# Attention pieces regrouped from six to five a batch, SyncE's transfers put in given order, K's transpose ahead of Q's, in a fused Linformer attention and feed-forward kernel

## The chip, the cores and the metric

One core of one Trainium2 chip. The metric is device time in microseconds (us) of one launch. The kernel before takes 488.2 us (median of four runs, 488.0 to 488.4). Two figures for one kernel below, such as 488.2 and 485.8 us, are the device time and the span of the profile, from the first to the last instruction; times inside a profile count from the start of its span. Each experiment was compared with the kernel before on the same chip and in the same rounds, so ratios are safer to compare than times of different experiments.

In the views, PE is TensorE (matrix products) and PEld its weight loads, DVE is VectorE, ACT is ScalarE. POOL (PoolE) and SP (SyncE) here mainly issue transfers, which 16 DMA engines carry out. "Issue" is the time for which the issuing engine is held; a transfer "lands" when its data has arrived.

## The reference

```python
# q, k, v: (8 batches, 8 heads, 1024, 64); E, F: (64, 1024); w_in: (512, 2048); w_out: (2048, 512)
k_proj = einsum('ks,bhsd->bhkd', E, k)          # 1024 positions -> 64
v_proj = einsum('ks,bhsd->bhkd', F, v)
attn   = softmax(q @ k_proj.T / sqrt(64))       # per head
x      = (attn @ v_proj), heads joined          # (8192, 512)
out    = relu(x @ w_in)**2 @ w_out              # (8192, 512)
```

## The kernel before

Each batch goes through two chunks of the feed-forward network: `f0` (16 steps of the first layer), `s0` (15 steps of the second), `f1`, `s1`, so 62 steps numbered n = 0 to 61. Batch 0 runs `f0 f1 s0 s1`. The second layer's matrix product uses 7 products with sums and differences (`s0` to `s3`, `T1` to `T4`) in place of 8. Attention of the next batch (`nxt`) is cut into pieces, and tables say before which step each piece is put:

```python
ORDERED = {mybir.EngineType.PE, mybir.EngineType.DVE, mybir.EngineType.Activation}
...
qkv_pool = ctx.enter_context(tc.tile_pool(name="qkv", bufs=1))     # one Q_sb, one K_sb, one V_sb
qt_pool  = ctx.enter_context(tc.tile_pool(name="qt", bufs=1))      # one qT
aps = ctx.enter_context(tc.tile_pool(name="aps", bufs=2, space=bass.MemoryType.PSUM))
...
def transpose_q(self):      # "Q's crossbar": a DMA transpose of 1 MB, SBUF to SBUF, issued by SyncE
    nc.sync.dma_start_transpose(out=self.qT[:], in_=self.Q[:].rearrange("p h c -> p (h c)"))
def copy_kp(self):          # after project(): two copies on VectorE, then "K's transpose", a small one
    ...
    nc.sync.dma_start_transpose(out=self.kT[:], in_=self.kp[:].rearrange("k h a d -> k (h a d)"))
...
with tc.manual_schedule(engines=ORDERED):
    def load_batch(b):      # three loads of 1 MB each on PoolE's queue
        if b < B:
            tiles = [load(n, src, b) for n, src in (("Q_sb", q), ("K_sb", k), ("V_sb", v))]
            return Attention(b, *tiles)
```

Engines in `ORDERED` get their instructions in the order in which the program names them. The others, here SyncE and PoolE, get the order that the scheduler of the kernel language settles when the kernel is built. Each of Q_sb, K_sb and V_sb has one buffer. So a batch's load of Q waits until the batch before has had its Q read by the crossbar, and its loads of K and V wait until the batch before has been projected on TensorE.

The softmax here doesn't subtract the row's maximum and nothing guards it: scores larger than these inputs give would overflow.

## Time and profile before

| | before |
|---|---|
| device time, median | 488.2 us |
| TensorE busy | 472.6 of 485.8 us |
| a middle batch | 57.60 us, TensorE busy throughout |
| the last batch, without attention | 55.7 us with the tail |

From the page of the kernel before: the span, the busy time of each engine, then TensorE's busy share and granted clock, in tenths, in 40 equal slices.

```profile
span 485.8 us, 8378 instructions
...
PE 472.6 (97%) x3614; PEld 292.3 (60%) x3614; DVE 315.4 (65%) x380; ACT 262.4 (54%) x414; POOL 33.2 (7%) x46
...
PE   4899999999999999999999999999999999999997
...
PEclk9999999999999999999999999999999999999999
```

The next view is the table of stretches: bounds, length, busy us (and instruction count) of the engines, the granted clock, the DMA share and GB/s. The rows are the end of batch 0, batch 1, and one middle batch.

```profile
core 0: us, PE busy (x) PEld busy (x) DVE busy (x) ACT busy (x) POOL busy (x), PEclk, DMA share, GB/s
52.00:83.48 31.48, 30.67 (x305) 23.37 (x305) 19.16 (x29) 13.75 (x20) 2.62 (x3) 1.00 0.99 171
83.48:143.75 60.27, 60.01 (x451) 36.56 (x449) 38.37 (x46) 33.61 (x52) 5.26 (x6) 1.00 0.87 155
201.35:258.95 57.60, 57.60 (x434) 35.56 (x432) 38.80 (x45) 31.94 (x50) 2.63 (x3) 1.00 0.53 106
```

First the timeline of SyncE, start and length of the issue of each transfer:

```profile
57.73 5.02 SPq L167 DMA_TRANSPOSE qT<-Q_sb  x1
62.81 1.25 SPq L185 DMA_TRANSPOSE kT<-kp  x1
...
79.29 12.77 SPq L167 DMA_TRANSPOSE qT<-Q_sb  x1
```

Then PoolE, with the idle time ahead of each issue and what ended it:

```profile
66.84 0.87 POOL L78 DMA_DIRECT2D Q_sb<-in_q_dram  x1 [34.43 <-DMA qT<-Q_sb]
67.70 0.88 POOL L78 DMA_DIRECT2D K_sb<-in_k_dram  x1
68.57 0.89 POOL L78 DMA_DIRECT2D V_sb<-in_v_dram  x1
96.24 0.88 POOL L78 DMA_DIRECT2D Q_sb<-in_q_dram  x1 [26.78 <-DMA qT<-Q_sb]
```

Batch 2's Q stands first in PoolE's queue and waits for batch 1's crossbar, and K and V stand behind it. Whether by intent or not, this keeps all three loads off the DMA engines while batch 1's crossbar runs. The DMA view of 57.7 to 66.4 us, the life of that crossbar, shows this: queue, packets and MB, share of the 16 DMA engines' time; then the crossbar's time from issue to landing.

```profile
q1 hardware_dynamic: 4672, 1.18, 85.9%
...
qT<-Q_sb SPq DMA_TRANSPOSE x1, 8.6
```

SyncE's queue (q1) has the DMA engines to itself, and the crossbar lands in 8.6 us. Last, TensorE at the first scores of batch 1, which need qT and kT:

```profile
65.19 1.03 PE L461 MATMUL ps_y<-T,hsq 128*128 128x256 bf16 x8
66.72 0.63 PE L201 MATMUL ps_att<-qT,kT 64*64 64x512 bf16 x8 [0.51 <-DMA kT<-kp]
```

The wait there is 0.5 us, and it is for kT, which SyncE issues behind Q's crossbar.

### The profile page before, as it was taken

To read this page: it belongs to the slowest core of one execution; us is meant where nothing else is said; L and a number is where in the kernel's file an instruction comes from. 1 tells how busy PE (TensorE), PEld (TensorE's weight loads), DVE (VectorE), ACT (ScalarE), POOL (GpSimd) and SP (SyncE) were. 2 spreads that over 40 slices of the span, in tenths; PEclk is the share of its full clock that TensorE was granted. 3 is DMA by queue.
4 is the path that set the end of the run, shared out by engine and by line. 5 is a ranking of instruction groups with operands and counts; after the bars stand their busy time and mean duration, and the time that the engine had idled before them with its cause. 6 is when DMAs were issued, how large, how long until landed. Compare 5 with 4: busy or idle time off the path is not lost.

```text
span 485.8 us, 8378 instructions
## 1 busy us (share of the span) xinstructions
PE 472.6 (97%) x3614; PEld 292.3 (60%) x3614; DVE 315.4 (65%) x380; ACT 262.4 (54%) x414; POOL 33.2 (7%) x46
## 2 busy tenths in 40 slices
PE   4899999999999999999999999999999999999997
PEld 2444677475574845757475665747557474666656
DVE  2478855566848568495765848566694856848383
ACT  2487445665727556355655467264672746645351
POOL 6330020010020000100010000200000000000000
PEclk9999999999999999999999999999999999999999
DMA  9999999997389124991149921893232102020202
GB/s 162 204 205 206 164 144 219 235 170 178 46 145 226 30 88 86 172 187 44 44 89 194 162 88 20 141 220 66 88 74 68 45 0 88 2 88 0 88 0 88
DMA packets 72501, 55.46 MB, mean 114 GB/s; under 512 B 33936, under 2 KB 64656, under 8 KB 72464
## 3 DMA queue, kind: packets, MB, share of 16 engines
q0 software_dynamic: 30336, 29.36, 38.5%
q1 hardware_dynamic: 42128, 25.56, 20.7%
q8 instruction: 28, 0.46, 0.4%
q14 instruction: 9, 0.07, 0.0%
HBM read 59.24 MB, written 16.78 MB: 156 GB/s over the span
## 4 chain that ended last, share of the span: by engine, by line
PE 85%; DMA 10%; ACT 2%; POOL 1%; issue 1%; DVE 0%; POOLq 0%; DVEq 0%
PE ps_h L441 39%; PE ps_y L461 23%; PE ps_z L461 11%; DMA V_sb<-in_v_dram 7%; PE ps_x L461 5%; DMA w_in<-in_moe_w_in_dram 2%; PE ps_att L216 2%; PE ps_kv L175 2%; PE ps_att L201 2%; DMA kT<-kp 1%; ACT h_relu L492 1%; PE ps_kv L176 0%; POOL K_sb L91 0%; DVE hsq L500 0%; ACT hsq L498 0%
## 5 line engine op out<-in xcount | busy, mean ns | idle before, releaser
L441 PE MATMUL ps_h<-xT,w_in 128*128 128x512 bf16 x1024 | 225.0, 379 | 0.2 <-DMA w_in<-in_moe_w_in_dram 0.2
L500 DVE TENSOR_TENSOR hsq<-h_relu 128x1024 bf16<-128x1024 f32 x123 | 150.2, 1222 | 67.4 <-ACT h_relu L492 66.8
L492 ACT ACTIVATE h_relu<-ps_h 128x512 f32<-128x512 f32 x256 | 150.6, 597 | 66.2 <-PE ps_h L441 65.7
L441 PEld LDWEIGHTS <-w_in 128*128 128x128 bf16 x1024 | 99.5, 98 | 118.2 <-issue 1.8
L461 PEld LDWEIGHTS <-s 128*128 128x128 bf16 x1024 | 98.4, 98 | 19.6 <-issue 8.1
L461 PEld LDWEIGHTS <-hsq 128*128 128x128 bf16 x768 | 73.2, 98 | 19.4 <-issue 3.0
L461 PE MATMUL ps_y<-T,s 128*128 128x256 bf16 x512 | 62.4, 273 | 0.1
L574 DVE TENSOR_TENSOR o_sb<-ps_z,p_b 128x512 f32<-128x512 f32 x16 | 11.1, 692 | 52.9 <-issue 25.7
L455 DVE TENSOR_TENSOR s<-hsq 128x1024 bf16<-128x1024 bf16 x64 | 43.6, 684 | 0.0
L570 ACT COPY o_sb<-ps_y 128x512 f32<-128x512 f32 x15 | 8.8, 585 | 55.4 <-PE ps_y L461 55.4
L235 DVE TENSOR_TENSOR xT<-ps_att,rs 128x1024 bf16<-128x1024 f32 x28 | 33.0, 1217 | 7.3 <-ACT rs L229 7.3
L461 PE MATMUL ps_y<-w_out,hsq 128*128 128x256 bf16 x256 | 34.5, 273 | 0.3 <-DVE hsq L500 0.3
L461 PE MATMUL ps_x<-w_out,hsq 128*128 128x256 bf16 x256 | 33.2, 273 | 0.0
L461 PE MATMUL ps_y<-T,hsq 128*128 128x256 bf16 x256 | 31.7, 272 | 0.0
L208 ACT ACTIVATE expT<-ps_att 128x1024 bf16<-128x1024 f32 x28 | 27.4, 1028 | 6.4 <-PE ps_att L201 6.4
L461 PE MATMUL ps_z<-T,s 128*128 128x256 bf16 x256 | 30.8, 273 | 0.0
L461 PE MATMUL ps_z<-w_out,s 128*128 128x256 bf16 x256 | 30.6, 273 | 0.0
L570 ACT COPY p_b<-ps_y 128x512 f32<-128x512 f32 (+1 forms) x17 | 9.5, 560 | 28.1 <-PE ps_y L461 28.0
L78 POOL DMA_DIRECT2D Q_sb<-in_q_dram x7 | 6.1, 876 | 263.2 <-DMA qT<-Q_sb 262.8
L574 DVE TENSOR_TENSOR o_sb<-ps_y,p_d 128x512 f32<-128x512 f32 (+1 forms) x17 | 11.2, 660 | 19.2 <-PE ps_y L461 19.2
L228 ACT ACTIVATE rs<-ps_att 128x1024 f32<-128x1024 f32 x14 | 14.3, 1023 | 14.6 <-PE ps_att L216 14.6
L455 DVE TENSOR_TENSOR s<-s,hsq 128x1024 bf16<-128x1024 bf16 x32 | 21.9, 687 | 0.5
(74 smaller groups left out, 239.3 us busy)
## 6 DMA issues: line engine op xcount, KB each, us to landing
out_dram<-o_sb SPq DMA_DIRECT2D x30, 512.0 KB, 3.3
K_sb<-in_k_dram POOLq DMA_DIRECT2D x7, 1024.0 KB, 17.3
V_sb<-in_v_dram POOLq DMA_DIRECT2D x7, 1024.0 KB, 22.4
Q_sb<-in_q_dram POOLq DMA_DIRECT2D x7, 1024.0 KB, 9.6
w_in<-in_moe_w_in_dram POOLq DMA_DIRECT2D x8, 256.0 KB, 13.7
w_out<-in_moe_w_out_dram POOLq DMA_DIRECT2D x4, 512.0 KB, 13.2
K_sb<-in_k_dram POOLq DMA_DIRECT2D x2, 512.0 KB, 7.8
V_sb<-in_v_dram POOLq DMA_DIRECT2D x2, 512.0 KB, 12.7
```

The source lines that it names most:

```text
L175: nc.tensor.matmul(ps[0:KP, :], lhsT=ET[:, i, :], rhs=kv[:, :, i, :], start=f, stop=l)
L201: nc.tensor.matmul(ps[o, bank, :], lhsT=self.kT[r, 2 * pr + j, :], start=True, stop=True, rhs=self.qT[r, NT * (2 * pr + j):NT * (2 * pr + ...
L208: nc.scalar.activation(e[:], self.ps["s", pr][:], AF.Exp, scale=SCALE)
L228: nc.scalar.activation(rs[:], self.ps["r", g][:], AF.Ln)
L235: nc.vector.tensor_tensor(out=self.xT[:, 2 * g + e].rearrange("p a n t -> p a (n t)"), in0=self.ps["v", g, e][:], in1=self.rs[g][:], op=AL ...
L441: nc.tensor.matmul(ps[:], lhsT=w_in_blk(cb, fb), rhs=xT[:, cb, :, 2 * ch:2 * ch + 2], start=(cb == 0), stop=(cb == NCB - 1),)
L455: nc.vector.tensor_tensor(out=s[o][:, js], in0=x, in1=y, op=op)
L461: nc.tensor.matmul(ps[tb] if len(ps) == 2 else ps[0][:, tb], lhsT=lhs[:, j, tb * P:(tb + 1) * P], rhs=rhs[:, j], start=first and n == 0 an ...
L492: nc.scalar.activation(r[:, n], ps[:], AF.Relu)
L500: multiply = lambda: nc.vector.tensor_tensor(out=o, in0=r[:], in1=r[:], op=ALU.mult)
L570: nc.scalar.copy(to[:, t], ps)
L574: nc.vector.tensor_tensor(out=to[:, t], in0=ps, in1=more[:, t], op=ALU.add)
```

## The change

Its intent: fewer switches between attention and feed-forward on TensorE; K's small transpose ahead of Q's large one; Q's crossbar after its load, at a place that the program gives. SyncE joins the engines in given order. The core of the diff, with cuts marked:

```diff
-ORDERED = {mybir.EngineType.PE, mybir.EngineType.DVE, mybir.EngineType.Activation}
+ORDERED = {
+    mybir.EngineType.PE, mybir.EngineType.DVE, mybir.EngineType.Activation, mybir.EngineType.SP,
+}
...
     PIECES = {
-        0: "transpose_q", 1: "copy_kp", 2: "copy_vp", 4: "copy_v_down",
-        24: "scores 0, scores 1, exponentials 0", 25: "exponentials 1",
-        27: "sums 0, values 0 0, reciprocals 0", 30: "values 0 1", 31: "normalize 0 0", 32: "normalize 0 1",
-        47: "scores 2, scores 3, exponentials 2", 48: "exponentials 3",
-        50: "sums 1, values 1 0, reciprocals 1", 53: "values 1 1", 54: "normalize 1 0", 55: "normalize 1 1",
+        1: "copy_kp", 2: "copy_vp", 4: "copy_v_down",
+        20: "scores 0, scores 1, exponentials 0", 21: "exponentials 1",
+        23: "sums 0, values 0 0, reciprocals 0", 26: "normalize 0 0",
+        28: "scores 2, scores 3, exponentials 2", 29: "exponentials 3",
+        47: "values 0 1, sums 1, reciprocals 1", 48: "normalize 0 1",
+        53: "values 1 0, values 1 1", 54: "normalize 1 0", 55: "normalize 1 1",
     }
     BATCH_1 = {
-        32: "project", 33: "copy_kp, transpose_q, copy_vp", 36: "copy_v_down",
+        33: "project", 34: "copy_kp, transpose_q, copy_vp", 37: "copy_v_down",
         46: "scores 0, scores 1, exponentials 0", 47: "exponentials 1",
...      # the rest of batch 1's pieces regrouped: seven places become six
-    BATCH_2 = {**PIECES, 1: "", 2: "", 4: "", 9: "project", 10: "copy_kp", 11: "copy_vp", 14: "copy_v_down"}
+    BATCH_2 = {
+        **PIECES, 1: "", 2: "", 4: "", 9: "project", 10: "copy_kp, transpose_q", 11: "copy_vp", 14: "copy_v_down",
+    }
     SECOND_HALF = {
-        1: "last_of_first", 7: "second_half 0 0", 9: "second_half 1 0, second_half 0 1",
+        1: "last_of_first", 7: "second_half 0 0", 9: "second_half 1 0", 10: "second_half 0 1",
...
                     if n == (35, 12, 1)[min(b, 2)]:
                         ahead = load_batch(b + 2)
+                    if b and n == 33 and ahead:
+                        ahead.transpose_q()
...      # also: one more held-back square in batch 0, later operand sums on VectorE
```

## The prediction

> **What bounds the kernel now.** TensorE: 97% of the 485.8 us span by the page, 85% of the chain that ended last, at clock 0.999. In the table of stretches the middle batches take 57.60 us, TensorE busy for all of it; VectorE (38.8) and ScalarE (31.9) have room. The last batch, without attention, takes 2 x 26.1 us, so attention costs 5.4 us a batch. Its matmuls account for 3.9 us (projection 1.73, scores 0.86, sums and values 1.30, start to start in the timeline). The other 1.5 us is changes of tile shape: 8 second-layer matmuls take 0.87 us alone and 0.96-0.98 beside a piece, so about 0.11 us a change, 13 a batch. The Trainium skill ("TensorEngine Tiling (Array Packing)", Key Properties) says that changing the tiling mode drains TensorE; the 0.1 us agrees in kind.
>
> **What the change does.**
> 1. Six attention places a batch become five ("values 0 1" joins "sums 1"; both "values" of group 1 and the next projection stand together): 13 changes of shape become 11, 0.23 us x 6 batches = 1.4 us. Batch 1 goes from seven places to six: 0.2.
> 2. Batch 1's projection comes one step later. Now TensorE stands 0.4 us there, at 52.0-52.7, for V's load (timeline). Gone.
> 3. Batch 1: SyncE now issues Q's crossbar (57.7, 5.0 us of issue) ahead of K's (62.8), and the scores wait for kT until 66.7: 0.5 us. With K first, kT lands near 60 and Q's crossbar, still bound by Q's load, near 65, a microsecond before it is wanted. Gone.
> 4. Opening batch: the second transposes of Q wait 0.4 us for Q's load at 29.8; a step later this goes, for one more change of shape: 0.3 net.
> 5. Costs. (a) Batch 2: Q's crossbar follows K's at about 95.7, takes 7 us to land, and the scores come four steps earlier, at about 102.3: waits 0.4 (0 to 0.8). (b) Scores 3 needs the PSUM buffer that "normalize 0 0" frees, which stands on VectorE behind an addition: free 2.1 us after p3's end, wanted at 2.06: 0.1 x 6. (c) Batch 1: "sums 1" waits for exponentials 3 behind a copy on ScalarE, "values 1 1" for "normalize 0 1": 0.5 together.
> 6. Q is loaded and turned half a batch earlier. PoolE's 263 us of waiting for the crossbar is off the chain; scores have 5 us to spare for kT (median landing 10.5): nothing.
> The reordered operands move VectorE work that has slack: nothing.
>
> Gains 1.4 + 0.2 + 0.4 + 0.5 + 0.3 = 2.8; costs 0.4 + 0.6 + 0.5 = 1.5; net 1.4 with rounding.
>
> **Prediction.** 486.7 us, 8 in 10 between 485.0 and 488.4. Faster by over 2%: 0.01; within 2%: 0.97; slower: 0.02.
>
> **What the profile would show.** Middle batches at 57.4-57.5 us, TensorE still busy throughout; five attention places a batch; in batch 1 no wait of the projection for V nor of the scores for kT, K's transpose issued first; a short wait of scores for qT in batch 2; perhaps a weight load of scores waiting for normalize once a batch. PoolE's wait stays large.
>
> **What would make it wrong.** SyncE in given order: a transpose waiting for a late load blocks the output stores, and through the two output buffers the additions, PSUM and TensorE. A crossbar amid loads, as at 79.3 now (12.8 us of issue), before batch 2's or 3's scores. More PSUM waits than I found: every batch then gives back more than its 0.23 us.

## The result

The changed kernel takes 511.0 us (median of four, 509.8 to 511.5) against 488.2 us: a ratio of 1.0464, 95% interval 1.0444 to 1.0484. A ratio here is the mean time of one kernel's fast runs over that of the other's of the same rounds, so not quite the ratio of the medians quoted. The prediction was 486.7 us, so it was wrong in direction and by far more than its range.

The page of the changed kernel:

```profile
span 509.5 us, 8379 instructions
...
PE 475.6 (93%) x3614; PEld 295.0 (58%) x3614; DVE 313.5 (62%) x380; ACT 263.1 (52%) x414; POOL 33.2 (7%) x46
...
PE   4899919991999999999999999999999999999997
...
PEclk9999967996999999999999999999999999999999
```

The loss is not spread: two slices of TensorE are nearly empty, in batches 0 and 1, and the clock dips beside each. The other slices look as before. The table of stretches, for the same stretches of work (the end of batch 0, batch 1, one middle batch; columns as in the table above):

```profile
52.00:96.00 44.00, 33.53 (x309) 24.54 (x307) 19.95 (x30) 13.91 (x20) 2.63 (x3) 0.84 0.88 146
96.00:168.72 72.72, 61.37 (x451) 37.10 (x449) 38.06 (x46) 33.92 (x52) 5.26 (x6) 0.93 0.73 131
226.10:283.48 57.38, 57.38 (x435) 35.64 (x432) 38.52 (x45) 32.13 (x50) 2.63 (x3) 1.00 0.59 113
```

Batch 0 ends 12.5 us later (96.00 against 83.48), and batch 1 takes 12.5 us longer (72.72 against 60.27). The middle batch takes 57.38 in place of 57.60 us: the regrouping gives what it was meant to give. Four such batches give 0.9 us and batch 6, from start to start in the chain of waits, gives 0.4 (398.41 to 453.94, against 374.33 to 430.22), so 12.5 + 12.5 - 1.3 = 23.7 us, which is the difference of the spans (509.5 - 485.8).

TensorE at the first scores of batch 1:

```profile
65.13 1.03 PE L467 MATMUL ps_y<-T,hsq 128*128 128x256 bf16 x8
76.43 1.07 PE L203 MATMUL ps_att<-qT,kT 64*64 64x512 bf16 x8 [10.26 <-DMA qT<-Q_sb]
77.43 1.89 PE L467 MATMUL ps_y<-T,hsq 128*128 128x256 bf16 x8
79.11 1.91 PE L467 MATMUL ps_y<-w_out,hsq 128*128 128x256 bf16 x8
...
126.08 1.07 PE L203 MATMUL ps_att<-qT,kT 64*64 64x512 bf16 x8 [11.09 <-DMA qT<-Q_sb]
```

TensorE reaches the same place at the same time as before (65.13 and 65.19 us) and then stands 10.3 us for qT; at batch 2's first scores it stands 11.1 us. Behind each wait the matmuls are slow: 8 of the second layer take 1.7 us from start to start, where they took 0.9. SyncE and PoolE, in that order:

```profile
57.64 1.74 SPq L187 DMA_TRANSPOSE kT<-kp  x1
59.51 14.74 SPq L169 DMA_TRANSPOSE qT<-Q_sb  x1
...
107.06 1.26 SPq L187 DMA_TRANSPOSE kT<-kp  x1
108.50 15.52 SPq L169 DMA_TRANSPOSE qT<-Q_sb  x1
```

```profile
55.68 0.88 POOL L80 DMA_DIRECT2D K_sb<-in_k_dram  x1 [22.68 <-PE ps_kv L178]
56.55 0.88 POOL L80 DMA_DIRECT2D V_sb<-in_v_dram  x1
76.85 0.88 POOL L80 DMA_DIRECT2D Q_sb<-in_q_dram  x1 [19.42 <-DMA qT<-Q_sb]
106.07 0.88 POOL L80 DMA_DIRECT2D K_sb<-in_k_dram  x1 [28.35 <-PE ps_kv L178]
107.14 0.89 POOL L80 DMA_DIRECT2D V_sb<-in_v_dram  x1 [0.20 <-issue]
```

SyncE issues Q's crossbar only 1.8 us later than before (59.51 against 57.73), but the issue lasts 14.7 us in place of 5.0. What is new is on PoolE, which the diff does not name: K and V of batch 2 go off at 55.7 and 56.6 us, as soon as the projection of batch 1 has read their buffers, where they used to go at 67.7 and 68.6 us, behind Q. The same happens for batch 3 at 106 us. The DMA view of 59.5 to 76.4 us, the life of this crossbar:

```profile
q0 software_dynamic: 1876, 1.89, 73.8%
q1 hardware_dynamic: 4829, 1.50, 49.8%
...
qT<-Q_sb SPq DMA_TRANSPOSE x1, 16.8
```

PoolE's loads (q0) and SyncE's transfers (q1) are now on the DMA engines together, and the crossbar lands in 16.8 us in place of 8.6. The Trainium skill ("DMA: Bandwidth & Descriptors", Issuing engines are not separate DMA queues) says that transfers started by different engines run on the same 16 DMA engines and interleave; these two views agree.

The built queues show the order of the loads on PoolE for batches 1 to 4:

```
before:   K V Q | Q K V | Q K V | Q K V
changed:  K V Q | K V Q | K V Q | Q K V
```

### The profile page after: what moved, and what is told of

Same layout as the page of the kernel before. It is cut to its first block, busy times and chain, and to the rows that moved or that the text cites. A ratio compares the mean times of both kernels' runs of the same rounds, so it can differ in the third digit from the quotient of the medians.

```text
span 509.5 us, 8379 instructions
## 1 busy us (share of the span) xinstructions
PE 475.6 (93%) x3614; PEld 295.0 (58%) x3614; DVE 313.5 (62%) x380; ACT 263.1 (52%) x414; POOL 33.2 (7%) x46
## 4 chain that ended last, share of the span: by engine, by line
PE 78%; DMA 3%; ACT 0%; issue 0%
PE ps_h L447 37%; PE ps_y L467 20%; PE ps_z L467 10%; PE ps_x L467 5%; DMA qT<-Q_sb 3%; PE ps_kv L177 2%; PE ps_att L218 2%; PE ps_att L203 2%; ACT h_relu L498 0%; ACT o_sb L646 0%; PE ps_kv L178 0%; ACT hsq L504 0%
## 5 line engine op out<-in xcount | busy, mean ns | idle before, releaser
L506 DVE TENSOR_TENSOR hsq<-h_relu 128x1024 bf16<-128x1024 f32 x123 | 150.2, 1222 | 77.0 <-ACT h_relu L498 76.3
L467 PEld LDWEIGHTS <-hsq 128*128 128x128 bf16 x768 | 74.9, 99 | 18.5 <-issue 3.6
L582 DVE TENSOR_TENSOR o_sb<-ps_z,p_b 128x512 f32<-128x512 f32 x16 | 11.1, 692 | 61.0 <-ACT p_b L578 38.0
L467 PE MATMUL ps_z<-T,s 128*128 128x256 bf16 x256 | 32.0, 280 | 0.0
L203 PE MATMUL ps_att<-qT,kT 64*64 64x512 bf16 x112 | 10.1, 427 | 21.4 <-DMA qT<-Q_sb 21.4
L461 DVE TENSOR_TENSOR s<-hsq,s 128x1024 bf16<-128x1024 bf16 x32 | 21.8, 683 | 0.0
L578 ACT COPY p_a<-ps_y 128x512 f32<-128x512 f32 (+1 forms) x17 | 9.4, 561 | 19.3 <-PE ps_y L467 19.3
```

Of the source, the lines that this page charges most:

```text
L203: nc.tensor.matmul(ps[o, bank, :], lhsT=self.kT[r, 2 * pr + j, :], start=True, stop=True, rhs=self.qT[r, NT * (2 * pr + j):NT * (2 * pr + ...
L461: nc.vector.tensor_tensor(out=s[o][:, js], in0=x, in1=y, op=op)
L467: nc.tensor.matmul(ps[tb] if len(ps) == 2 else ps[0][:, tb], lhsT=lhs[:, j, tb * P:(tb + 1) * P], rhs=rhs[:, j], start=first and n == 0 an ...
L506: multiply = lambda: nc.vector.tensor_tensor(out=o, in0=r[:], in1=r[:], op=ALU.mult)
L578: nc.scalar.copy(to[:, t], ps)
L582: nc.vector.tensor_tensor(out=to[:, t], in0=ps, in1=more[:, t], op=ALU.add)
```

## The experiments

**Theory.** With SyncE in given order, the scheduler puts K and V of batches 2 and 3 ahead of Q on PoolE, which it still orders itself. They then share the DMA engines with Q's crossbar, the crossbar takes twice as long, and TensorE waits. **Rival 1:** the new places of the attention pieces ask for qT too early. **Rival 2:** K's transpose, and SyncE's order as such, hold Q's crossbar back. Two further questions: does the price go with the bytes loaded beside the crossbar, and what part of the loss is the clock? Here are all runs; the landing times are those of batch 1's and batch 2's crossbar, and a dash means not of interest.

| run | device us, median | ratio to before | crossbar landings, us | TensorE's waits for qT or kT, us |
|---|---|---|---|---|
| changed kernel | 511.0 | 1.046 | 16.8, 17.5 | 10.3, 11.1 |
| after_sp_free | 488.3 | 1.001 | 8.5, - | 1.3, 2.6 (kT) |
| before_sp_given | 499.7 | 1.024 | 18.1, 7.6 | 9.7 |
| after_pool_given | 487.0 | 0.998 | 8.3, 6.7 | 1.2 |
| before_kv_early | 499.4 | 1.023 | 17.0, 7.1 | 9.4 (kT) |
| before_pool_given | 488.4 | 1.000 | 8.3, - | 0.2 (kT) |
| after_half_kv (wrong result) | 497.3 | 1.018 | 10.7, 10.5 | 3.7, 2.1 |
| after_filled | 509.4 | 1.043 | 16.4, 18.7 | most filled |
| after_filled_longer | 508.5 | 1.042 | 17.3, 18.7 | most filled |
| after_pool_later | 486.5 | 0.996 | 8.3, 6.7 | 0.5 |

### after_sp_free: the change without SyncE in given order

```diff
-    mybir.EngineType.PE, mybir.EngineType.DVE, mybir.EngineType.Activation, mybir.EngineType.SP,
+    mybir.EngineType.PE, mybir.EngineType.DVE, mybir.EngineType.Activation,
```

> The changed kernel with SyncE again left to the scheduler; everything else of the change stays. Built, PoolE's queue then has Q ahead of K and V for batches 2 and 3, as in the kernel before. Theory (crossbar shares the DMA engines with K's and V's loads, which came forward in PoolE's queue): the two waits for qT (10.3 and 11.1 us) vanish, 486 to 488 us, clock 0.999, PoolE's batch-2 K load comes after Q's crossbar (66 us or later). Rival 1 (the new places of the attention pieces want qT too early): both waits stay, about 510 us. Rival 2 (K's transpose in front of Q's on SyncE): 486 to 488 us as well, since Q's goes first again.

Measured: 488.3 us (486.2 to 491.3), ratio 1.0011 (0.9967 to 1.0056). Batch 2's K load is back behind Q, at 69.1 us, the crossbar lands in 8.5 us, and no matmul waits for qT. All the moved pieces are still there, so rival 1 alone cannot make the loss. Rival 2 stays open, since SyncE's order went back too. Two waits for kT that nobody expected appear in the profile, which is of the slowest of the four launches (491.3 us, clock 0.995; the two quickest took 486.2 and 487.2 us at clock 1.0). The first, 1.3 us, is for a K transpose that stands behind Q's crossbar on SyncE, and shows why one would want K's first. The second, 2.6 us, is not: that K transpose goes out at 96.2 us with no crossbar ahead of it, beside loads of Q, K and V issued at 95.2 to 97.2 us, and lands after 10.2 us, where batch 1's took 3.9. TensorE behind that second wait:

```profile
106.50 1.07 PE L201 MATMUL ps_att<-qT,kT 64*64 64x512 bf16 x8 [2.58 <-DMA kT<-kp]
107.50 2.86 PE L465 MATMUL ps_z<-T,s 128*128 128x256 bf16 x16
```

### before_sp_given: the kernel before with only SyncE in given order

```diff
-ORDERED = {mybir.EngineType.PE, mybir.EngineType.DVE, mybir.EngineType.Activation}
+ORDERED = {
+    mybir.EngineType.PE, mybir.EngineType.DVE, mybir.EngineType.Activation, mybir.EngineType.SP,
+}
```

> The kernel before, with SyncE in given order and nothing else. Built, PoolE's queue then has K and V of batch 2 ahead of Q. Theory: the first wait for qT comes back without any moved attention piece: Q's crossbar at about 59 us lands 15 us or more after its issue, TensorE stands about 10 us at 66 us, and the time is 498 to 503 us; the second wait may be missing, since Q of batches 2 and 3 stand ahead of K and V there. Rival 1 (places of the pieces): 487 to 489 us. Rival 2 (K's transpose first on SyncE): a wait, but Q's crossbar lands in 7 to 8 us.

Measured: 499.7 us, ratio 1.0235 (1.0214 to 1.0256). One line of the diff gives half of the loss. K's load of batch 2 goes at 55.8 us, the crossbar issued at 58.8 us lands after 18.1 us, and the scores wait 9.7 us. Batch 2's crossbar meets no K or V (they go at 106.9 us, behind Q) and lands in 7.6 us, without a wait. This points to the loads that the line lets come forward; the next two runs test that. Rival 2 as stated (a late but quick crossbar) does not fit the 18.1 us.

### after_pool_given: the change with PoolE in given order as well

```diff
     mybir.EngineType.PE, mybir.EngineType.DVE, mybir.EngineType.Activation, mybir.EngineType.SP,
+    mybir.EngineType.Pool,
...
-                tiles = [load(n, src, b) for n, src in (("Q_sb", q), ("K_sb", k), ("V_sb", v))]
-                return Attention(b, *tiles)
+                src = {"Q_sb": q, "K_sb": k, "V_sb": v}
+                names = ("K_sb", "V_sb", "Q_sb") if b == 1 else ("Q_sb", "K_sb", "V_sb")
+                t = {n: load(n, src[n], b) for n in names}
+                return Attention(b, t["Q_sb"], t["K_sb"], t["V_sb"])
```

> The changed kernel with SyncE's order kept, and PoolE in given order too: batch 1 K, V, Q, every later batch Q, K, V, so that K and V of batches 2 and 3 queue behind the Q load that waits for the crossbar. Theory: crossbars land in 7 to 8 us, the two waits shrink from 10.3 and 11.1 us to about 1 us each, 486.5 to 489 us, clock 0.99 or more. Rivals 1 and 2: SyncE's order and the places are as in the changed kernel, so about 510 us.

Measured: 487.0 us (486.0 to 488.4), ratio 0.9982 (0.9960 to 1.0003). From its timelines of SyncE and PoolE, and its list of TensorE's waits (us in total, times, longest):

```profile
56.85 1.31 SPq L188 DMA_TRANSPOSE kT<-kp  x1
58.28 4.85 SPq L170 DMA_TRANSPOSE qT<-Q_sb  x1
...
67.12 0.88 POOL L81 DMA_DIRECT2D Q_sb<-in_q_dram  x1 [34.59 <-DMA qT<-Q_sb]
67.99 0.88 POOL L81 DMA_DIRECT2D K_sb<-in_k_dram  x1
```

```profile
PE ps_att L204 <- DMA qT<-Q_sb: 1.2, 1, 1.2
```

SyncE's order and the pieces are those of the changed kernel; only the loads wait their turn. The crossbar's issue is 4.9 us again, and the two long waits are gone. So neither rival makes the loss without the early loads. A slow crossbar is not always paid for: batch 3's, issued here at 115.5 us, met loads and took 17.6 us to land, and no scores waited for it.

### before_kv_early: the converse, in the kernel before

The kernel before with PoolE in given order, and `names = ("K_sb", "V_sb", "Q_sb")` for every batch in the loader shown above. SyncE stays free.

> The kernel before, SyncE free as it was, with PoolE alone in given order: K, V, Q in every batch, so that batch 2's K and V go off as soon as batch 1's projection has read their buffers (55 us), in front of batch 1's crossbar. Theory: the crossbar at 57.7 us takes 15 us or more, K's transpose goes out behind it, TensorE stands about 10 us at 66 us: 497 to 502 us with a clock dip. Rivals 1 and 2: neither the places nor SyncE's order moved, so 487 to 489 us.

Measured: 499.4 us, ratio 1.0232 (1.0215 to 1.0249). Its timeline of SyncE, and its list of waits:

```profile
57.96 14.88 SPq L167 DMA_TRANSPOSE qT<-Q_sb  x1
72.90 1.25 SPq L185 DMA_TRANSPOSE kT<-kp  x1
```

```profile
PE ps_att L201 <- DMA kT<-kp: 9.4, 1, 9.4
```

Half of the loss, batch 1's wait, appears in a kernel that has nothing of the change, with Q's crossbar first on SyncE. The wait is put down to kT, since kT is issued last here, behind the 14.9 us of the crossbar's issue: the name of the waiting buffer differs, the cause does not.

### before_pool_given: control

As before_kv_early, with the order that the queue had anyway (batch 1 K, V, Q; then Q, K, V).

> Control for the run in which K and V came early in the kernel before: PoolE in given order as there, but in the order that its queue had anyway (batch 1 K, V, Q, later Q, K, V). Theory and rivals alike: 487 to 489 us, crossbar at 57.7 us landing in about 7 us. If given order of PoolE were itself the cost, 497 us or more.

Measured: 488.4 us, ratio 0.9995 (0.9980 to 1.0011). Given order of PoolE costs nothing by itself; K and V early cost the 11 us.

What the two converse runs do not show is batch 2's wait, the other half of the loss. With the pieces in their old places, batch 2's crossbar goes off at 97.5 us (before_sp_given) or 86.7 us (before_kv_early), ahead of batch 3's loads (105.7 and 104.5 us), and lands in 7.6 and 7.1 us. In the changed kernel its new place puts it at 108.5 us, right behind those loads (106.1 and 107.1 us) and shortly ahead of the scores. So for batch 2 the early loads were needed (after_pool_given), but by these runs not enough without the new places: there rival 1 falls as the sole cause, not as a part of it.

### after_half_kv: does the price go with the bytes?

```diff
+        n = H // 2 if b in (2, 3) and name != "Q_sb" else H
+        if n < H:
+            nc.vector.memset(t[:, n:H], 0.0)
-        nc.gpsimd.dma_start(t[:], rows(src, b))
+        nc.gpsimd.dma_start(t[:, 0:n], rows(src, b)[:, 0:n])
```

> The changed kernel, wrong on purpose: of batches 2 and 3 only four of eight heads of K and V are loaded, the rest is set to zero on VectorE; all queues keep their order. Theory (Q's crossbar ends about when the loads beside it end, a cost that goes with their bytes): landing of the two crossbars falls from 17.5 us to 10 to 13 us, the two waits from 10.3 and 11.1 us to 3 to 7 us each, 494 to 502 us. Rival (a fixed price of a crossbar that meets any load): landing and waits stay, 508 to 512 us.

Measured: 497.3 us, ratio 1.0182 (1.0163 to 1.0202); the result is wrong, as intended. With half of K and V beside them the crossbars land in 10.7 and 10.5 us, against 16.8 and 17.5 with all of them. From the DMA view of its batch 1:

```profile
qT<-Q_sb SPq DMA_TRANSPOSE x1, 10.7
```

A fixed price falls. Half of the bytes is here also half of the packets, so the run does not tell these two apart. One side effect: the added fills on VectorE held up a square, and TensorE stood 2.1 us for it in batch 1 just ahead of the scores, so the second wait of 2.1 us is short by about that much.

### after_filled and after_filled_longer: how much of the loss is the clock?

```diff
+                if (b, n) in ((0, 46), (1, 20)):
+                    ps = ffn_psum("ps_fill")
+                    for _ in range(42):                  # after_filled_longer: 44 if b == 0 else 58
+                        nc.tensor.matmul(ps[:], lhsT=ET[:, 0:2, :], rhs=ET[:], start=True, stop=True)
```

> The changed kernel with 42 idle 128x512 matmuls (9.1 us at full clock) put in front of the two groups of scores that wait, so that TensorE is busy through most of both waits; nothing else differs. Theory: the waits as such stay (the crossbars land when they did), but the half clock after them goes, and with it what the trace of the changed kernel shows as slow matmuls there: 2.7 us after the first wait and 1.8 us after the second, so 505.5 to 508.5 us at clock 0.99 or more. Rival (the matmuls after the waits are slow for another reason, such as the loads still running): 510 to 512 us, the 8 second-layer matmuls after the first scores still at about 1.7 us.

Measured: 509.4 us (508.3 to 510.7), ratio 1.0426 (1.0404 to 1.0449): a miss, a little above the range. The first place did what was expected: 8 matmuls behind it take 0.9 us. At the second, 42 were too few, TensorE still stood 3.2 us, and the 16 matmuls behind it took 3.3 us, as slow as in the changed kernel. So the second place was tried again:

> The filled version again with 44 idle matmuls in front of the first scores and 58 in front of batch 2's, since 42 left 3.2 us of standing before the second and the matmuls behind it stayed slow. Theory: now neither group is followed by slow matmuls (8 second-layer matmuls take 0.87 to 0.98 us, 16 take 1.75 to 1.85), clock 0.999, and the time is 505.5 to 508.5 us, 1.036 to 1.041 of the time before against 1.0464 for the changed kernel. Rival (the matmuls after the waits are slow for another reason): those after the second group stay slow, 3.1 to 3.4 us for 16.

Measured: 508.5 us (507.3 to 509.1), ratio 1.0422 (1.0399 to 1.0445), clock 0.999; the ratio is again just above the expected 1.036 to 1.041. Its timeline of TensorE at the second place:

```profile
111.86 12.68 PE L697 MATMUL ps_fill<-ET 128*128 128x512 bf16 x58
124.47 0.63 PE L203 MATMUL ps_att<-qT,kT 64*64 64x512 bf16 x8
125.03 1.92 PE L467 MATMUL ps_z<-T,s 128*128 128x256 bf16 x16
```

The scores and the 16 matmuls behind them take 2.32 us here (124.47 to 126.79), where they take 4.09 in the changed kernel (126.08 to 130.17): 1.8 us. At the first place the same comparison, from the scores to the end of 24 matmuls, gives 5.88 - 3.19 = 2.7 us. So the slow matmuls come from standing still, not from the loads: batch 3's load of Q starts right behind the scores here too (124.8 us; 126.6 in the changed kernel). Of these 4.5 us the profiles show 3.3 saved (509.5 - 506.2) and the medians 2.5: in this run batch 2's crossbar landed in 18.7 us in place of 17.5, which gives 1.2 us back. Whether the idle matmuls slow the crossbar or whether that is its ordinary spread stays open.

The Trainium skill ("TensorE: Matmul & The Clock Gate", HAM oscillation) says to avoid TensorE gaps over about 3.4 us, as the clock then falls to half. The trace agrees for the long waits: the granted clock, the third column from the right, is 0.50 from 70 to 82 us in the changed kernel.

```profile
70.00:77.00 7.00, 0.57 (x8) 0.22 (x8) 0.00 (x0) 0.00 (x0) 0.15 (x1) 0.50 1.19 267
77.00:82.00 5.00, 5.00 (x30) 3.28 (x23) 0.00 (x0) 2.54 (x3) 0.73 (x1) 0.50 0.71 90
```

Shorter stands were enough too: 3.2 us in after_filled, and 2.6 us in after_sp_free (with a hole of 0.3 us just before it), where the clock is 0.50 from 106.5 to 108 us and 16 matmuls take 2.7 us. Stands of 1.1 us (first place of after_filled_longer) and 1.3 us (after_sp_free) were not followed by slow matmuls.

### after_pool_later: a version that beats both

From after_pool_given, batch 1's first scores one step later, since they still waited 1.2 us:

```diff
-        46: "scores 0, scores 1, exponentials 0", 47: "exponentials 1",
+        47: "scores 0, scores 1, exponentials 0", 48: "exponentials 1",
```

> The version with PoolE and SyncE both in given order, batch 1's scores 0 and 1 one step later (47 and 48 in place of 46 and 47), since they waited 1.2 us for qT at 66 us. Theory: that wait falls to 0.2 to 0.4 us and nothing else moves: 485.5 to 487.5 us, 0.9982 of the time before falling to 0.995 to 0.998. If exponentials 1 then hold the buffer that scores 3 needs, the gain is lost: 486.5 to 487.5 us.

Measured: 486.5 us (486.1 to 487.1) against 489.1 us before on the same chip, ratio 0.9960 (0.9945 to 0.9975) over five rounds. The wait is 0.5 us, a little above the expected 0.2 to 0.4. The interval is clear of 1: the change, with the loads held in place and this one step, is worth 0.4%.

## Why the prediction was wrong, point by point

- **The bound (TensorE) and the gain of the regrouping: right.** Predicted 57.4 to 57.5 us for a middle batch, measured 57.38 against 57.60. I built the estimate from 0.11 us for each change of tile shape. The Trainium skill ("TensorEngine Tiling (Array Packing)", Key Properties) says that a change of tiling mode drains TensorE; 8 matmuls taking 0.96 to 0.98 us beside a piece and 0.87 us elsewhere fit that in kind; no view shows the drain itself.
- **Batch 1's projection and the opening (points 2 and 4): not shown.** TensorE's waits for V's load at the projection and for Q's load in the opening are not in the profile after. But before_pool_given, with every piece in its old place, has neither of them either, so no run shows that the change took them away.
- **The failing step is point 3, repeated in 5a: "With K first, kT lands near 60 and Q's crossbar, still bound by Q's load, near 65", and "takes 7 us to land".** What failed is the landing time of the crossbar: TensorE was to wait 0 and 0.4 us for it and waited 10.3 and 11.1. K's transpose did go first, but landed at 67.1 us (57.64 + 9.5), not near 60, and Q's crossbar was issued 1.8 us later than before. It landed at 76.3 us, after 16.8 us, and batch 2's took 17.5. I took the landing time from a trace in which PoolE's queue kept the DMA engines clear, and carried it into a kernel whose PoolE queue is built anew. The trace held the counter-example: the crossbar at 79.3 us, amid loads, took 12.8 us to issue and 16.4 to land, and I used it only as a caution. It cost nothing there, since batch 2's scores came only at 106.2 us.
- **Point 6, "nothing", is where I should have looked.** I saw that Q is loaded and turned earlier, judged PoolE's 263 us of waiting to be off the chain, and did not ask what K and V do when they no longer stand behind Q. That wait was idle time of an engine off the critical path, and it was also what kept the loads apart from the crossbar.
- **The costs 5b and 5c.** 5b is right in kind and too small to matter: the weight loads of scores wait for "normalize" six times, 0.2 us each, and the middle batches still gain 0.22 us. The waits of 5c are not in the profile: no wait stands ahead of batch 1's sums or values in the list of TensorE's waits.
- **The sum.** The two waits add 10.3 - 0.5 and 11.1 us, the half clock behind them 2.7 and 1.8, together 25.4. The regrouped middle batches and batch 6 give back 1.3. That makes 24.1 us, where 23.7 were measured; the difference of 0.4 us lies in batch 1, whose gains I did not take apart. With the loads held back the rest of the sum was near: after_pool_given took 487.0 us and after_pool_later 486.5, where 486.7 had been predicted.
- **"What would make it wrong" named a crossbar amid loads**, but I put no number or probability on it. With it, the range would have had to reach past 500 us.

Why the scheduler turned PoolE's order round is inferred, not shown: with SyncE free it is Q, K, V, with SyncE given it is K, V, Q for batch 2, in the kernel before as in the changed one. Its reasons were not looked at, and stay open.

## What to carry to other kernels

An engine left to the scheduler is part of every change: after giving one engine a fixed order, compare the built queues of the engines that were not named, above all those that issue transfers. A duration read from a trace holds for the company the transfer had there, so before reusing it ask which loads can start earlier now, and what used to stop them. Where a wait of an idle engine keeps two transfers apart, make that order explicit, as after_pool_given does.

## What the Trainium skill lacked or had wrong

- "DMA: Bandwidth & Descriptors", Rules for kernel authors, says "A transpose next to ordinary DMAs needs nothing". That is about correct results; it lacks the price: beside 2 MB of loads a 1 MB transpose landed in 16.4 to 18.7 us, beside 1 MB in 10.5 to 10.7, and alone in 6.7 to 8.6.
- The same page (Latency and other measured facts) gives 261 GB/s for one kernel's DMA transposes. Here 1 MB took 6.7 to 8.6 us from issue to landing with no load beside it, so about 120 to 160 GB/s, setup included; in the view of 57.7 to 66.4 us of the kernel before the DMA engines moved 200 to 225 GB/s while most of its packets ran.
- "TensorE: Matmul & The Clock Gate" (HAM oscillation) names gaps over about 3.4 us. Here gaps of 3.2 us (16 matmuls in 3.3 us in place of 1.8) and of 2.6 us with a hole of 0.3 us just before it (16 matmuls in 2.7 us) were followed by half clock; 1.1 and 1.3 us were not.
- "TensorEngine Tiling (Array Packing)", Key Properties, gives no size for the drain at a change of mode: about 0.11 us a change here, if all of the extra time is the drain, and 0.22 us a batch for two fewer.
- No page read here says that giving one engine's order by hand can reorder the queues left to the scheduler: in before_sp_given this alone cost 2.35%.
